# The first four up products of a fused attention and two-layer network, moved into the hand-pinned opening order

## The chip, the cores and the metric

The kernel runs on one core of a Trainium2 chip. The metric is the device time of one execution in microseconds (us), as the median of several runs. The core has a matrix engine (PE in the profile, with its weight loads listed as PEld), a vector engine (DVE), a scalar engine for activations (ACT), a general engine (POOL), and queues that start DMA transfers (SPq). Each engine works through its own list of instructions in order, and waits on semaphores that the others raise.

## The reference

Attention between `x` (4 batches, 8 heads, 512 rows, 64 columns) and a `state` of 32 rows per head goes into two gated layers, each of 512 to 2048 to 512 features:

```python
a = softmax(scale * x @ state.T)            # per head; xread below
xread = a @ state
sread = softmax(scale * state @ x.T) @ x    # state reads x
x = concat([xread, sread])                  # 4 * (512 + 32) tokens, 512 features
h = x @ moe_w_in;   y = (h - tanh(h)) @ moe_w_out
h = y @ moe2_w_in;  out = (h * tanh(log1p(exp(min(h, 20))))) @ moe2_w_out
```

Two things of it shape the kernel. All inputs are stored as 64-bit floats, so each weight arrives as pairs of 32-bit words and has to be converted on the chip. And `xread @ w_in` is computed as `a @ (state @ w_in)`: the small product `state @ w_in` is made first, per batch, and the softmax weights `a` multiply it directly.

## The kernel before, in words

**Layer one.** A batch has 512 tokens; they are the moving columns of nearly every matmul (128x512). The 2048 hidden features are 16 tiles `t` of 128. An *up product* of tile `t` (`up_x`, line 525) makes `h`, 128 features by 512 tokens, in one PSUM bank: for each of two halves `j` of the heads, three matmuls (`mm3p`, line 503) on rounded operands split in a high and a low part, `swh`/`swl` being the split of `state @ w_in` and `ath`/`atl` that of the transposed softmax weights `a`. So an up product is six matmuls. `elem1` (line 515) then makes `t = h - tanh(h)`: a Tanh on ACT, a subtraction on DVE, and, from tile 3 on, a further split in `gh` (ACT) and `gl` (DVE). A *down product* of tile `t` (`down_x`, line 548) adds `t` times `w_out` into four accumulators, PSUM banks a0 to a3; tiles 0 to 2 of batch 0 (`PLAIN = 3`) use plain 32-bit matmuls, `acc<-t,w`, and later tiles the three-matmul form.

**Weights.** Each load brings 512 KB of 64-bit weights into one of six staging buffers (`st` three times, `wide` three times). A conversion (`conv_steps`, line 189) is a pair on ACT, a Prelu that writes `w` and a Copy that writes `r`, and then one SCALAR_TENSOR_TENSOR on DVE that joins them in `w`. The Copy frees the staging buffer, and the next load is issued only then (`load_next`, line 174). Layer one needs 16 conversions of `w_in` (key `("w1i", c, k)`, chunk `c` of four feature tiles, piece `k`) and 16 of `w_out` (`("w1o", t)`). They are loaded alternately after the first five.

**State times w_in.** For chunk 0 it is made feature tile by feature tile (`sw_first`, line 489): eight small matmuls `swp<-w,sbt` of 128 columns, the high part `swh` by two ACT copies, the low part `swl` by two DVE subtractions (`sw_first_lo`). For later chunks it is one piece (`sw`, line 475) of 512 columns, which needs all four converted pieces of the chunk.

**Order.** The work of the opening is written out by hand in `FIRST_STEPS` (line 34): a letter and a number for a step, for instance `w3` for the next step of converting piece 3, `f2` and `g2` for the high and low part of `state @ w_in` of feature tile 2, `h1`/`l1` for the parts of `a`. Up to the bar `|` each instruction of PE, ACT and DVE is pinned behind the one before it on its engine (class `Pinned`; its line 59 issues nearly every instruction, so nearly every row of the profile says L59). Behind the bar only a floor holds: nothing may go ahead of the last pinned instruction, and a scheduler orders the rest by its own rules when the program is built. The main loop (line 958) then issues, per step `i`, the up product of step `i`, its side work, and the down product of step `i - 3`:

```python
    for s in range(16):
        at(s, lambda s=s: conv_w1o(s))
        if s < 11:
            at(s, lambda s=s: conv_w1i((s + 5) // 4, (s + 5) % 4))
            if s % 4 == 2:
                at(s, lambda s=s: sw(0, s // 4 + 1))
```

So step `s` converts `w_out` tile `s` and `w_in` piece `s + 5`, and `sw(0, 1)` comes at step 2. Piece 4, which is (1, 0), is converted by the last steps `w4 w4 w4` of the table.

**Banks.** Up products use h0 and h1 in turn. The small products of the opening take their bank from a rotating list (`side_bank`, line 129), and step `z` moves the place in that list.

Of the kernel before, what the change touches and what calls it, by code (L numbers as in the profile page):

```python
# [29 lines left out]

FIRST_LOADS = "s0123wwt4567wwww"
FIRST_STEPS = """
    k4 s0 x0 X0 x1 X1 x2 X2 x3 X3 w0 w0 c0 C0 C1 k2 w0 t0 m0 t1 w1 w1 f0 b0 p0 P0 m1 e0 p1 P1 b1
    p2 e1 P2 u0 p3 P3 v0 y0 k6 w2 u1 v1 w2 h0 z2 q1 y1 h1 g0 l0 w1 l1 Q0 Q1 | f1 g1 w2 f2 g2
    w3 w3 w3 f3 g3 w4 w4 w4
"""
BLOCKS = [4, 4, 4, 3, 2]

# [31 lines left out]
def attention_moe_kernel(  # L72
# [11 lines left out]
    B, H, S, D = x.shape  # L84
# [5 lines left out]
    T = S + NS  # L90
# [9 lines left out]
    TE, AC, V = (Pinned(e, order) for e in (nc.tensor, nc.scalar, nc.vector))  # L100
# [18 lines left out]
    def put(*units):  # L119
        for u in units:  # L120
            if u.slot is None:
                halves.append(u)
            else:
                free.append(u.slot)

    ps_n = [0]
    banks = ["s0", "s1", "a0", "a1", "a2", "a3", "h0", "h1"]
# [129 lines left out]
    X, A, AT = {}, {}, {}  # L257
# [20 lines left out]
    def xt_t(b, k):  # L278
        P["x", b, k] = ps = side_bank("xtp")
        for r in range(4):  # L280
            TE.transpose(
                out=ps[:, r * 128:(r + 1) * 128],
                in_=X[b, k].t[:, r * 128:(r + 1) * 128],
                identity=ident,
            )

    def xt_c(b, k):
        XT[b, k] = get("xt")
        evac(XT[b, k].t, P.pop(("x", b, k)), 0 if b else k)
# [157 lines left out]
    def at_a_hi(b, j):  # L447
        ps = side_bank("atp")
        a = A.pop((b, j))
        for r in range(4):  # L450
            TE.transpose(
                out=ps[:, r * 128:(r + 1) * 128],
                in_=a.t[:, r * 128:(r + 1) * 128],
                identity=ident,
            )
        put(a)
        h = get("ath", F32R)
        last[0] = AC.activation(out=h.t, in_=ps, func=ACTF.Copy).ins
        AT.setdefault(b, []).append((h, ps))

    def at_a_lo(b, j):
        h, ps = AT[b][j]
        l = get("atl", F32R)
        V.tensor_tensor(out=l.t, in0=ps, in1=h.t.bitcast(F32), op=ALU.subtract)
        AT[b][j] = (h, l)
# [7 lines left out]
    SW = {}  # L473
# [29 lines left out]
    def mm3p(o, lh, ll, rh, rl, start, stop):  # L503
        TE.matmul(out=o, lhsT=lh, rhs=rh, start=start, stop=False)
        TE.matmul(out=o, lhsT=lh, rhs=rl, start=False, stop=False)
        TE.matmul(out=o, lhsT=ll, rhs=rh, start=False, stop=stop)
# [4 lines left out]
    def h_bank(tags):  # L511
        h_n[0] += 1
        return psum.tile([128, 512], F32, tag=tags[h_n[0] % len(tags)], name="h")

    def elem1(key, h):
        t = get("t")
        last[0] = AC.activation(out=t.t, in_=h, func=ACTF.Tanh).ins
        V.tensor_tensor(out=t.t, in0=h, in1=t.t, op=ALU.subtract)
        if key[0] == 0 and key[1] < PLAIN:
            G[key] = t  # L520
            return
        G[key] = split(t.t, name="g")
        put(t)

    def up_x(b, t):
        h = h_bank(["h0", "h1"])
        c, f = t // 4, (t % 4) * 128
        for j in range(2):
            wh, wl = SW[b, c, j]
            ah, al = AT[b][j]  # L530
            mm3p(h, wh.t[:, f:f + 128], wl.t[:, f:f + 128], ah.t, al.t, j == 0, j == 1)
        if t % 4 == 3:
            for j in range(2):
                put(*SW.pop((b, c, j)))
        if t == NT - 1:
            for p in AT.pop(b):
                put(*p)
        elem1((b, t), h)

    def acc_bank(i, tags=("a0", "a1", "a2", "a3")):  # L540
        return psum.tile([128, 512], F32, tag=tags[i % len(tags)], name=f"acc{i}")
# [115 lines left out]
    def up_2(n, t, i_tail):  # L657
        N = 128 * len(blocks[n])
        h = h_bank(HT)[:, :N]
        c, f = t // 4, (t % 4) * 128  # L660
        for k in range(KD):
            wh, wl = W2I[c, k]
            yh, yl = YB[n][k]
            mm3p(
                h, wh.t[:, f:f + 128], wl.t[:, f:f + 128], yh.t[:, :N], yl.t[:, :N],
                k == 0, k == KD - 1,
            )
        if t == NT - 1:
            for p in YB.pop(n):
                put(*p)  # L670
        if n == 0 and done[0] < len(late):
            e, r = get("e"), get("r")
            m, rr = e.t[:, :N], r.t[:, :N]
        else:
            e, r = None, stage.tile([128, 1024], F32, tag="st", name="er")
            m, rr = r[:, :N], r[:, 512:512 + N]
        AC.activation(out=m, in_=h, func=ACTF.Exp)
        if i_tail is not None:
            elem2_hi(*i_tail)
        V.tensor_scalar(out=m, in0=m, scalar1=E20, scalar2=None, op0=ALU.min)  # L680
        V.scalar_tensor_tensor(
            out=m, in0=m, scalar=2.0, in1=m, op0=ALU.add, op1=ALU.mult
        )
        AC.activation(out=rr, in_=m, func=ACTF.Ln, bias=2.0)
        AC.activation(out=rr, in_=rr, func=ACTF.Exp, scale=-1.0)
        E2[n, t] = (e, r, m, rr, h, N)

    def elem2(n, t, i_tail):
        e, r, m, rr, h, N = E2[n, t]
        w = get("w2")  # L690
        ww = w.t[:, :N]
        V.scalar_tensor_tensor(
            out=ww, in0=m, scalar=2.0, in1=rr, op0=ALU.add, op1=ALU.mult
        )
        if i_tail is not None:
            elem2_lo(*i_tail)
        V.tensor_tensor(out=rr, in0=h, in1=rr, op=ALU.mult)
        V.scalar_tensor_tensor(
            out=m, in0=ww, scalar=2.0, in1=m, op0=ALU.subtract, op1=ALU.mult
        )  # L700
        V.scalar_tensor_tensor(
            out=m, in0=m, scalar=-1.0, in1=rr, op0=ALU.mult, op1=ALU.mult
        )
        put(w)

    def elem2_hi(n, t):
        e, r, m, rr, h, N = E2[n, t]
        gh = get("gh", F32R)
        AC.activation(out=gh.t[:, :N], in_=m, func=ACTF.Copy)
        G["2", n, t] = (gh, get("gl", F32R))  # L710

    def elem2_lo(n, t):
        e, r, m, rr, h, N = E2.pop((n, t))
        gh, gl = G["2", n, t]
        V.tensor_tensor(
            out=gl.t[:, :N], in0=m, in1=gh.t[:, :N].bitcast(F32), op=ALU.subtract
        )
        if e is not None:
            put(e, r)
# [150 lines left out]
    st = {}  # L870
    for key in FIRST_LOADS:
        if key in "st":
# [18 lines left out]
            first[f] = conv_steps(("w1i", f // 4, f % 4))  # L891
        W1I[f // 4, f % 4] = next(first[f])

    def skip_banks(n):
        ps_n[0] += n

    steps = {
        "x": lambda k: xt_t(0, k), "X": lambda k: xt_c(0, k), "s": lambda j: state_t(j, st[j]),
# [1 line left out]
        "m": lambda j: sc_max(0, j), "b": lambda j: sc_sub(0, j), "e": lambda j: sc_exp(0, j),  # L900
        "u": lambda j: nm_sum(0, j), "v": lambda j: nm_rec(0, j), "y": lambda j: nm_mul(0, j),
        "h": lambda j: at_a_hi(0, j), "l": lambda j: at_a_lo(0, j), "f": sw_first,
        "g": sw_first_lo, "z": skip_banks,
        "w": conv_first, "k": keep_warm, "p": lambda k: xt_t(1, k), "P": lambda k: xt_c(1, k),
        "q": sc_m, "Q": lambda j: sc_c(1, j),
    }
# [18 lines left out]
    def up(q):  # L925
        if q[0] == "x":
            up_x(q[1], q[2])
        elif q[0] == "s":
            up_s(q[1])
        else:  # L930
            if q[2] == 0:
                if q[1] == 0:
                    pre = nc.scalar.preload_act_table_set("natural_log_exp_and_others").ins
                    order(pre, last[0])
                    AC.last, V.last = pre, None
                    AC.floor = V.floor = None
                    AC.on = V.on = True
                y_block(q[1])

    def down(q):  # L940
        if q[0] == "x":
            down_x(q[1], q[2])
        elif q[0] == "s":
            down_s(q[1])
        else:
            down_2(q[1], q[2])
# [10 lines left out]
    for i in range(len(seq) + 2):  # L957
        marks.append([e.recent for e in engines])
        q = seq[i] if i < len(seq) else None
        prev = [seq[i - k][1:] if start["2"] <= i - k < len(seq) else None for k in range(3)]  # L960
        if q:
            up(q)
        if prev[0]:
            up_2(*prev[0], prev[2])
        elif prev[2]:
            elem2_hi(*prev[2])
        if prev[1]:
            elem2(*prev[1], prev[2])
        elif prev[2]:
            elem2_lo(*prev[2])  # L970
        if prev[0] and q[2] >= NT - 6:
            y_block(q[1] + 1, YSPARE)
        for f in side.pop(i, []):
            f()
        while low < len(seq) and low <= i - ahead(i):
            down(seq[low])
            low += 1
        pinned = AC.on, V.on
        AC.on = V.on = False
        late_conv(i)  # L980
        AC.on, V.on = pinned
# [33 lines left out]
```

## Time and profile before

| what | us |
|---|---|
| time, median of 3 runs (lowest, highest) | 745.51 (744.6, 745.74) |
| time of the profiled execution | 744.79 |
| span of the profiled execution | 743.0 |
| PE busy in the span | 729.0 (98%) |
| DVE busy | 542.8 (73%) |
| ACT busy | 413.4 (56%) |

The span runs from the first to the last instruction of the program; the execution's own time is a little longer. Busy time overlaps between engines. A row of the timeline gives the start, the length, the engine, the line, the operation, what is written and read, the shape, how many records were merged, and in brackets how long the engine had stood idle before it and which engine and tile ended that. The 32-bit matmuls `acc<-t,w`, `swp` and `sbp` leave two records for each instruction.

### The profile page before, as it was taken

The page shows a single profiled execution, that of the slowest core. Times are in us where ns is not written, and L with a number is a line of the kernel's source. Part 1 is how long each engine was busy: PE and PEld are TensorE (multiplying, and loading weights), DVE is VectorE, ACT ScalarE, POOL GpSimd, SP SyncE. Part 2 cuts the span into 40 slices and gives each one's busy share as a digit, 9 for nine tenths or more (in the row PEclk, how much of TensorE's full clock was granted, in tenths as well). Part 3 has the DMA queues.
Part 4 walks back from the last instruction along what each step waited for, and adds up shares of the span by engine and source line. Part 5 has one row for each costly group of instructions (what it writes and reads, how often), then busy time and mean ns, then how long its engine had stood idle before and what let it go on. Part 6 is the DMA issues. An engine that isn't in the chain of part 4 may idle for free.

```text
span 743.0 us, 10599 instructions
## 1 busy us (share of the span) xinstructions
PE 729.0 (98%) x4144; PEld 591.9 (80%) x4144; DVE 542.8 (73%) x1006; ACT 413.4 (56%) x770; POOL 6.6 (1%) x14
## 2 busy tenths in 40 slices
PE   8899999999999999999999999999999999999997
PEld 6467876788767898778888888888888888898996
DVE  5899655834466343777698988878788788888896
ACT  6998544534555443787674654535454454545563
POOL 0000010001000000000000000000000000000000
PEclk9999999999999999999999999999999999999999
DMA  9984110002100110453310000100010000100100
GB/s 295 328 298 141 58 56 1 2 24 78 43 29 13 47 57 1 142 169 115 114 56 1 1 1 16 42 0 1 0 57 1 0 1 1 56 1 2 43 1 28
DMA packets 17169, 43.14 MB, mean 58 GB/s; under 512 B 2656, under 2 KB 6752, under 8 KB 17120
## 3 DMA queue, kind: packets, MB, share of 16 engines
q1 hardware_dynamic: 16480, 40.38, 16.3%
q0 software_dynamic: 640, 2.10, 0.9%
q8 instruction: 32, 0.52, 0.3%
q14 instruction: 17, 0.14, 0.1%
HBM read 38.01 MB, written 4.46 MB: 57 GB/s over the span
## 4 chain that ended last, share of the span: by engine, by line
PE 89%; ACT 6%; DVE 3%; DMA 1%; issue 0%; SPq 0%; ACTq 0%
PE acc L59 46%; PE h L59 37%; ACT w L59 2%; PE swp L59 2%; ACT r L59 2%; PE srd L59 1%; DMA x<-in_x_dram 1%; ACT swh L59 1%; PE xtp L59 1%; PE sct L59 1%; DVE swl L59 1%; ACT t L59 1%; PE atp L59 1%; PE e2p L59 1%; DVE gl L59 0%
## 5 line engine op out<-in xcount | busy, mean ns | idle before, releaser
L59 PE MATMUL h<-yl,wh 128*128 128x512 f32 (+2 forms) x320 | 114.5, 358 | 0.0
L59 PE MATMUL h<-yh,wl 128*128 128x512 f32 (+2 forms) x320 | 114.4, 358 | 0.0
L59 PE MATMUL h<-yh,wh 128*128 128x512 f32 (+2 forms) x320 | 114.4, 358 | 0.0
L59 PE MATMUL acc<-wh,gl 128*128 128x512 f32 x288 | 112.6, 391 | 0.0
L59 PE MATMUL acc<-wl,gh 128*128 128x512 f32 x288 | 112.5, 391 | 0.0
L59 PE MATMUL acc<-wh,gh 128*128 128x512 f32 x288 | 112.5, 391 | 0.0
L59 ACT ACTIVATE er<-er 128x512 f32<-128x512 f32 (+2 forms) x136 | 75.7, 557 | 42.8 <-DVE er L59 40.6
L59 PE MATMUL acc<-gh,wh 128*128 128x512 f32 x244 | 98.9, 405 | 0.0
L59 PE MATMUL acc<-gh,wl 128*128 128x512 f32 x244 | 95.7, 392 | 0.0
L59 PE MATMUL acc<-gl,wh 128*128 128x512 f32 x244 | 95.5, 391 | 0.0
L59 ACT ACTIVATE er<-h 128x512 f32<-128x512 f32 (+2 forms) x68 | 35.5, 522 | 103.7 <-PE h L59 102.6
L59 DVE SCALAR_TENSOR_TENSOR er<-er 128x512 f32<-128x512 f32 (+2 forms) x136 | 81.3, 598 | 4.7
L59 PEld LDWEIGHTS h<-yl,wh 128*128 128x128 f32 x320 | 60.3, 188 | 9.4 <-DVE yl L59 0.7
L59 PEld LDWEIGHTS h<-yh,wh 128*128 128x128 f32 x320 | 60.3, 188 | 9.1 <-ACT yh L59 0.3
L59 PEld LDWEIGHTS h<-yh,wl 128*128 128x128 f32 x320 | 60.3, 188 | 7.4
L59 PEld LDWEIGHTS acc<-wh,gl 128*128 128x128 f32 x288 | 54.0, 188 | 12.0 <-DVE gl L59 0.7
L59 PEld LDWEIGHTS acc<-wh,gh 128*128 128x128 f32 x288 | 54.1, 188 | 11.1 <-ACT t L59 0.8
L59 PEld LDWEIGHTS acc<-wl,gh 128*128 128x128 f32 x288 | 54.1, 188 | 10.3
L59 PEld LDWEIGHTS acc<-gh,wh 128*128 128x128 f32 x244 | 45.8, 188 | 16.0 <-issue 4.4
L59 DVE TENSOR_TENSOR t<-h,t 128x512 f32<-128x512 f32 x48 | 33.0, 687 | 34.9 <-ACT t L59 34.8
L59 DVE TENSOR_SCALAR er<-er 128x512 f32<-128x512 f32 (+2 forms) x68 | 25.8, 379 | 44.3 <-ACT er L59 44.1
L59 PEld LDWEIGHTS acc<-gl,wh 128*128 128x128 f32 x244 | 45.9, 188 | 10.4 <-issue 2.1
(145 smaller groups left out, 1233.7 us busy)
## 6 DMA issues: line engine op xcount, KB each, us to landing
st<-in_moe_w_in_dram SPq DMA_DIRECT2D x27, 512.0 KB, 4.3
st<-in_moe_w_out_dram SPq DMA_DIRECT2D x22, 512.0 KB, 3.8
wide<-in_moe_w_out_dram SPq DMA_DIRECT2D x10, 512.0 KB, 4.9
out_dram<-wide SPq DMA_DIRECT2D x16, 256.0 KB, 2.2
wide<-in_moe_w_in_dram SPq DMA_DIRECT2D x5, 512.0 KB, 6.0
x<-in_x_dram SPq DMA_DIRECT2D x8, 256.0 KB, 5.8
x<-in_x_dram POOLq DMA_DIRECT2D x6, 256.0 KB, 3.1
wide<-in_x_dram POOLq DMA_DIRECT2D x2, 256.0 KB, 3.2
```

Source lines behind the costliest of these rows:

```text
L59: i = fn(*args, **kw)
```

## The change

The four up products of tiles 0 to 3 of batch 0 leave the main loop, which now starts its up products at step 4, and become steps of the pinned table: `U` opens an up product and issues its first half, `V` issues its second half, `T` issues the Tanh chain. Tiles 0 and 1 keep the banks h1 and h0; tiles 2 and 3 take the accumulators' banks a2 and a3. The remaining steps of chunk 0 (`f1` to `g3`) and the conversion of piece (1, 0) are pinned too, the bar moves to the end of the table, and the step `z` now names the next bank instead of skipping some. `up_x` is cut in two helpers with the same matmuls.

```diff
-    p2 e1 P2 u0 p3 P3 v0 y0 k6 w2 u1 v1 w2 h0 z2 q1 y1 h1 g0 l0 w1 l1 Q0 Q1 | f1 g1 w2 f2 g2
...
+    p2 e1 P2 u0 p3 P3 v0 y0 k6 w2 u1 v1 w2 h0 z0 q1 y1 z5 h1 g0 l0 U0 w1 l1 w3 w3 z2 f1 V0 w2 g1 T0
...
+    z4 f2 w3 U1 V1 g2 z2 f3 T1 U2 V2 g3 T2 U3 V3 Q0 Q1 T3 w4 w4 w4 |
...
     def up_x(b, t):
         h = h_bank(["h0", "h1"])
+        for j in range(2):
+            up_half(b, t, h, j)
+        up_end(b, t, h)
+
+    def up_half(b, t, h, j):
         c, f = t // 4, (t % 4) * 128
-        for j in range(2):
-            wh, wl = SW[b, c, j]
-            ah, al = AT[b][j]
-            mm3p(h, wh.t[:, f:f + 128], wl.t[:, f:f + 128], ah.t, al.t, j == 0, j == 1)
+        wh, wl = SW[b, c, j]
+        ah, al = AT[b][j]
+        mm3p(h, wh.t[:, f:f + 128], wl.t[:, f:f + 128], ah.t, al.t, j == 0, j == 1)
+
+    def up_end(b, t, h):
         if t % 4 == 3:
             for j in range(2):
-                put(*SW.pop((b, c, j)))
+                put(*SW.pop((b, t // 4, j)))
...
-    def skip_banks(n):
-        ps_n[0] += n
+    def up_first(t):
+        H[t] = acc_bank(t) if t > 1 else h_bank(["h0", "h1"])
+        up_half(0, t, H[t], 0)
+
+    H = {}
+
+    def next_bank(i):
+        ps_n[0] = i + len(banks) - 1
...
-        "g": sw_first_lo, "z": skip_banks,
+        "g": sw_first_lo, "z": next_bank, "U": up_first,
+        "V": lambda t: up_half(0, t, H[t], 1), "T": lambda t: up_end(0, t, H[t]),
...
-        if q:
+        if q and i >= 4:
             up(q)
```

Two places show what the built programs make of this. The first is PE's list around the first down product, `acc_502` to `acc_505` being the four accumulators; before:

```order
L59 MATMUL acc_502<-t,w 128x512
L59 MATMUL acc_503<-t,w 128x512
L59 MATMUL h<-ath,swh 128x512
L59 MATMUL h<-atl,swh 128x512
L59 MATMUL h<-ath,swl 128x512
L59 MATMUL h<-ath,swh 128x512
L59 MATMUL h<-atl,swh 128x512
L59 MATMUL h<-ath,swl 128x512
L59 MATMUL acc_504<-t,w 128x512
L59 MATMUL acc_505<-t,w 128x512
L59 MATMUL swp<-w,sbt 32x512 x8
```

The same place now, `acc_402` being the up product of tile 3 in bank a3:

```order
L60 MATMUL acc_402<-ath,swl 128x512
L60 MATMUL acc_502<-t,w 128x512
L60 MATMUL acc_503<-t,w 128x512
L60 MATMUL acc_504<-t,w 128x512
L60 MATMUL acc_505<-t,w 128x512
L60 MATMUL swp<-w,sbt 32x512 x8
L60 MATMUL acc_502<-t,w 128x512
L60 MATMUL h<-ath,swh 128x512
L60 MATMUL h<-atl,swh 128x512
L60 MATMUL acc_503<-t,w 128x512
```

The up product of tile 3 stood inside the first down product and is now ahead of it; the work ahead of the `swp` of chunk 1 is the same in both lists. Behind it, one more product of the second down product comes after the next up product has begun.

The second place is ACT's list from the two copies of `ath` on, where `w` and `r` are the Prelu and the Copy of a conversion; before:

```order
L59 ACTIVATE ath<-atp 128x512 x2
L59 ACTIVATE scs<-sct 128x2x128 x2
L59 ACTIVATE w<-wide 128x512
L59 ACTIVATE swh<-swp 128x128 x2
L59 ACTIVATE r<-wide 128x512
L59 ACTIVATE w<-wide 128x512
L59 ACTIVATE r<-wide 128x512
L59 ACTIVATE t<-h 128x512
L59 ACTIVATE swh<-swp 128x128 x2
L59 ACTIVATE w<-wide 128x512
L59 ACTIVATE swh<-swp 128x128 x2
L59 ACTIVATE r<-wide 128x512
```

The same place now, `acc_390` and `acc_402` being the up products of tiles 2 and 3:

```order
L60 ACTIVATE ath<-atp 128x512 x2
L60 ACTIVATE w<-wide 128x512
L60 ACTIVATE r<-wide 128x512
L60 ACTIVATE swh<-swp 128x128 x2
L60 ACTIVATE t<-h 128x512
L60 ACTIVATE swh<-swp 128x128 x4
L60 ACTIVATE t<-h 128x512
L60 ACTIVATE t<-acc_390 128x512
L60 ACTIVATE scs<-sct 128x2x128 x2
L60 ACTIVATE t<-acc_402 128x512
L60 ACTIVATE gh<-t 128x512
L60 ACTIVATE w<-wide 128x512
```

The second conversion in these rows, that of piece (1, 0), stood ahead of the first Tanh and now stands behind the fourth Tanh and `gh`; all later conversions follow it, eight pairs without anything between them.

## Rows read from the trace of the kernel before

**Rows 1.** Waits of PE, whole span: total us, times, longest.
```profile
PE swp L59 <- DVE w L59: 2.4, 2, 1.6
PE h L59 <- DVE t L59: 1.3, 1, 1.3
PE h L59 <- ACT swh L59: 0.3, 1, 0.3
```
**Rows 2.** Windows: us, busy of each engine, granted clock, DMA share, GB/s.
```profile
20.00:57.00 37.00, 34.18 (x200) 20.46 (x199) 32.95 (x60) 36.93 (x75) 0.00 (x0) 1.00 0.90 308
738.00:740.00 2.00, 1.02 (x5) 0.52 (x3) 0.69 (x1) 0.60 (x1) 0.00 (x0) 1.00 0.07 27
740.00:743.00 3.00, 0.00 (x0) 0.00 (x0) 0.00 (x0) 0.00 (x0) 0.00 (x0) 0.67 0.42 157
```
**Rows 3.** Timeline of PE from 3 to 69 us.
```profile
3.46 1.98 PE L59 MATMUL sbp<-ident,stt 128*64 128x128 f32 x16
...
21.30 0.40 PE L59 MATMUL h<-ath,swl 128*128 128x512 f32 x1
22.52 0.45 PE L59 MATMUL swp<-w,sbt 64*32 64x128 f32 x16 [0.82 <-DVE w L59]
23.21 0.72 PE L59 MATMUL swp<-w,sbt 64*32 64x128 f32 x16 [0.24 <-PE swp L59]
25.21 0.47 PE L59 MATMUL h<-ath,swh 128*128 128x512 f32 x1 [1.28 <-DVE t L59]
...
28.02 1.88 PE L59 MATMUL acc<-t,w 128*128 128x512 f32 x4
...
32.93 1.09 PE L59 MATMUL swp<-w,sbt 64*32 64x512 f32 x16
...
36.28 0.50 PE L59 MATMUL h<-ath,swh 128*128 128x512 f32 x1 [0.34 <-ACT swh L59]
...
38.27 1.09 PE L59 MATMUL sbp<-ident,stt 128*64 128x128 f32 x16
...
68.50 1.09 PE L59 MATMUL swp<-w,sbt 64*32 64x512 f32 x16 [1.55 <-DVE w L59]
```
**Rows 4.** Timeline of ACT from 19 to 34 us.
```profile
19.42 0.60 ACT L59 ACTIVATE ath<-atp 128x512 fp32r<-128x512 f32 x1 [1.07 <-PE atp L59]
...
21.87 0.68 ACT L59 ACTIVATE w<-wide 128x512 f32<-128x512 f32 x1
...
23.01 0.60 ACT L59 ACTIVATE t<-h 128x512 f32<-128x512 f32 x1
23.49 0.46 ACT L59 ACTIVATE swh<-swp 128x128 fp32r<-128x128 f32 x2
...
25.21 0.73 ACT L59 ACTIVATE w<-st 128x512 f32<-128x512 f32 x1
25.77 0.74 ACT L59 ACTIVATE r<-st 128x512 uint32<-128x512 uint32 x1
...
33.37 0.74 ACT L59 ACTIVATE gh<-t 128x512 fp32r<-128x512 f32 x1
33.88 0.80 ACT L59 ACTIVATE w<-st 128x512 f32<-128x512 f32 x1
```
**Rows 5.** Timeline of DVE from 23 to 69 us.
```profile
23.98 0.49 DVE L59 TENSOR_TENSOR swl<-swp,swh 128x128 fp32r<-128x128 f32 x2
24.38 0.68 DVE L59 TENSOR_TENSOR t<-h,t 128x512 f32<-128x512 f32 x1
...
27.66 0.69 DVE L59 SCALAR_TENSOR_TENSOR w<-w,r 128x512 uint32<-128x512 uint32 x1 [0.43 <-ACT r L59]
...
67.66 1.29 DVE L59 SCALAR_TENSOR_TENSOR w<-w,r 128x512 uint32<-128x512 uint32 x2
```
**Rows 6.** DMA from 20 to 57 us: rate in 40 slices; issues, KB, us to landing.
```profile
GB/s 403 381 244 244 350 186 275 248 319 270 239 221 261 425 425 425 416 399 416 372 354 297 279 368 345 297 199 204 226 252 314 297 301 239 363 350 283 345 159 323
...
wide<-in_moe_w_out_dram SPq DMA_DIRECT2D x9, 512.0 KB, 4.9
st<-in_moe_w_in_dram SPq DMA_DIRECT2D x6, 512.0 KB, 5.7
```

More of the change, by code (lines that the diff above doesn't have):

```diff
@@ L35 @@
     k4 s0 x0 X0 x1 X1 x2 X2 x3 X3 w0 w0 c0 C0 C1 k2 w0 t0 m0 t1 w1 w1 f0 b0 p0 P0 m1 e0 p1 P1 b1
-    p2 e1 P2 u0 p3 P3 v0 y0 k6 w2 u1 v1 w2 h0 z2 q1 y1 h1 g0 l0 w1 l1 Q0 Q1 | f1 g1 w2 f2 g2
-    w3 w3 w3 f3 g3 w4 w4 w4
+    p2 e1 P2 u0 p3 P3 v0 y0 k6 w2 u1 v1 w2 h0 z0 q1 y1 z5 h1 g0 l0 U0 w1 l1 w3 w3 z2 f1 V0 w2 g1 T0
+    z4 f2 w3 U1 V1 g2 z2 f3 T1 U2 V2 g3 T2 U3 V3 Q0 Q1 T3 w4 w4 w4 |
 """
```

## The prediction

> **What bounds the kernel now.** I read the page first: PE is busy for 98% of the span, so time can only come from PE's few waits or be lost in new ones. The list of PE's waits over the whole span names them [rows 1], and the timeline of PE shows where they lie [rows 3]: 0.82 and 0.24 us before the two `swp` at 22.5 and 23.2 us, 1.28 before the `h` at 25.21, 0.34 at 36.28, and 1.55 before the `swp` at 68.50. These five sum to 4.23 us; the first three, 2.34 us, lie where the change works. The reader should then look at the other engines in that stretch, for a wait of PE is only the late end of something. From 20 to 57 us ACT is busy 36.93 of 37.00 us, while PE has 34.18 [rows 2]. ACT bounds this stretch: it has the conversions of all first-layer weights to do, and it has no hole. PE's waits here are ACT's order showing through. Whoever changes that order must ask first whether ACT gets a hole.
>
> **The change part by part.** No matmul, activation or vector instruction is added or removed; a few merged rows differ, not the work. Split helpers and the new bank step cost no instruction, so these edits cost 0. The two up products in banks a2 and a3 add one wait: the first down product may write there only when the Tanh chain of tiles 2 and 3 has read them. By the walk below that chain is through at 28.7 us and the down product starts at 32.4, so this wait is covered by 3.7 us; it would cost only if the chain came later than the weight.
>
> What counts is the order. ACT now stands, in pinned order, behind each step of a ping-pong: PE's up product, ACT's Tanh, DVE's subtraction, and, because DVE's list puts the conversion of piece 3 behind the first subtraction, PE's next `swp`. Nothing may fill ACT's waits, since all other conversions are behind the table. I walk the new lists with durations of rows, starting where nothing has moved:
>
> The `ath` copy is at 19.42 and the up product of tile 0 ends at 21.30 + 0.40 = 21.70 as before [rows 3, 4]. Tanh, 0.60 long [rows 4], to 22.3. Subtraction, 0.68 [rows 5], to 23.0; the joining instruction behind it starts 0.60 after it did and takes 0.69 [rows 5], to 23.65. The `swp` of feature tile 3, 0.45 [rows 3], to 24.15. Two `swh` copies, 0.46 [rows 4], to 24.65, the second Tanh overlapping them, to 25.1. Its subtraction ahead of the `swl` pair, 0.68 and 0.49 with an overlap of 0.1 as at 23.98 [rows 5], to 26.25. PE has meanwhile done the rest and now needs four more matmuls for tile 3; by the 0.23 us from one to the next and 0.40 for the last, to 27.3. Tanh to 27.95, subtraction to 28.7, `gh`, after which ACT is free 0.52 later (33.37 to 33.88 [rows 4]): 29.25.
>
> So the conversion of piece (1, 0) begins at 29.25; before it began at 21.87 [rows 4]. From 20.0 to 29.25 ACT has a conversion pair (1.12, two steps of 0.56 [rows 4]), six small copies (three times 0.33), four Tanh (four times 0.49), two `scs` (0.54) and `gh` (0.52): 5.1 us of work in 9.25, thus a hole of some 4.1 us in an engine that had none.
>
> What PE does meanwhile: its matmuls end at 27.3, and the first down product needs `w_out` tile 0, the second conversion in the new order. Four steps of 0.56 from 29.25, the last 0.7 long, end at 31.65; DVE's 0.69 ends at 32.35; PE starts at 32.4. That is a new wait of about 5.1 us. The joins on DVE are not the bound: with 1.12 between Copies and 0.60 to 0.69 each they keep up.
>
> Then PE does four products of about 0.9 (28.02: two in 1.88 [rows 3]) until 36.0, and meets the `swp` of chunk 1, which needs pieces (1, 0) to (1, 3): the seventh pair in the new list. Its Copy starts at 29.25 + 13 x 0.56 = 36.5, ends 37.2, joined at 37.95: PE goes on at 38.0 after 2 us of waiting. Before, the same `swp` stood at 32.93 with the same work ahead of it, so PE is 5.1 us late here. Next, ACT copies `swh` only after nine pairs and a Prelu, at 39.9, with another Copy between the two: the second ends at 41.55, PE's `h` starts at 41.7 after another 1.8. With six matmuls and one product more, the `sbp` that was at 38.27 [rows 3] comes at 44.0: 5.7 us late.
>
> From there to the `swp` at 68.50 PE has the same work, and before it waited 1.55 there. The weight it waited for was joined at 67.66 [rows 5], kept late by DVE's list. PE now arrives at 66.95 + 5.7, about 72.6 (0.9 sooner at the `swp`, which stands four matmuls earlier in its list), so some 4 us lie between that join and PE even if DVE were no earlier. I count the 1.55 as gained. What costs it if the cover goes: DVE later by 4 us.
>
> Moved DMAs: each Copy releases the next load, so the load behind piece (1, 0) is issued about 30.5 instead of 23.16, and it is the load of piece (1, 3). Loads take 4.9 to 5.7 us to land here [rows 6], so it lands between 35.4 and 36.2, and ACT wants it at 36.0. This is the tightest place: from no cost to 0.2. The following loads are asked for every 1.12 us, which is 524 KB / 1.12 us = 468 GB/s, while no slice of this stretch shows more than 425 [rows 6]. At 425 a load takes 1.23, 0.1 behind ACT with each; at the mean of 308 [rows 2] it would take 1.7, 0.6 behind with each, over the two or three loads that matter before PE's `h` up to 1.5 us. I take 0.1, nearest to the slices in which the queue is full, and keep 0 and 1.5. The SP queue holds nothing else then, so nothing is delayed behind a waiting load.
>
> The sum: 5.7 late, less 1.55, is +4.15; with 0.1 for the loads +4.25. ACT's hole of 4.1 us says the same in another way. The profiled execution took 744.79, so 749.0; it lies 0.72 below the median of the runs shown, from which it would be 749.8. I forecast 749.4.
>
> **The clock.** The granted clock is 1.00, its level of 2.4 GHz, in the stretches shown with PE at work; at the very end, PE having stopped in the stretch from 738 to 740, it falls: 0.67 as the mean of the last three us, so its lower level within them [rows 2]. A gap of 5 us like the new one occurs nowhere inside the run (the longest listed is 1.6 us [rows 1]), so no row shows whether it would fall there. The Trainium skill, in TensorE: Matmul & The Clock Gate, section "HAM oscillation — how this bites in real kernels", says that a long wait between bursts of matmuls puts the clock back to half and lets the next burst run cold; by that rule the gap would cost more than itself. The price from rows: the 16 records of `sbp` took 1.98 at the start and 1.09 later [rows 3], a factor of 1.8, which I take for the lower level though no row gives the clock there. Four products would then take 6.6 from 32.4, to 39.0 instead of 36.0, of which 2 fall into the wait for the `swp`; that ends 1.9 later at 40.9, the next product at 42.5, against 41.7: 0.8 us more. If the clock rises again during the four products, nothing; if it stays low through the next up product and the product behind it, 0.8 x 2.3 = 1.8 on top, 2.6 in all.
>
> **The rivals.**
> 1. The clock falls in the gap and costs: +0.8, from just above 0 to 2.6, thus 750.2. For it: the fall at the end of the run; against: the next two waits, 2 and 1.8 us, take most of it.
> 2. Loads come late: ACT then waits for transfers in its row of bare conversions; up to +1.5, typical +0.8, thus 750.2. For it: 468 GB/s asked; against: the six loads ahead of that of piece (1, 3) have long landed.
> 3. On the other side: the pinned up products fill PE's holes and no new wait takes their place. All five waits go, 4.23 us: 744.79 - 4.23 = 740.6. It needs the conversion of (1, 0) to start early: since each us that ACT starts later is one us for PE, break-even is at 29.25 - 4.25 = 25.0, which would take round trips of half the length that the rows show. For it only that PE does have the up products to do in its 2.34 us of holes; against it ACT's 36.93 of 37.
> 4. The change is neutral: ACT's hole is partly filled and what PE loses is given back at 68.5: 745.5. Against it: the pinned list leaves nothing to fill with.
>
> **How the numbers follow.** Forecast 53%, rival 1 18%, rival 2 15%, rival 3 6%, rival 4 8%. A measurement of this kernel tells about 0.2%, 1.5 us, from no change. Slower takes the first three and a little of the fourth's spread, 0.87; same 0.07; faster 0.06. The range leaves out rivals 3 and 4 and reaches, above, to the forecast with 2.6 more: 746.9 to 752.3, where the lower end stands for round trips 2.5 us shorter than I walked.
>
> **What would show it.** Right: an idle time of some 5 us of PE before the first `acc<-t,w`, ended by DVE's `w`; two more, near 2 us, before the `swp` of chunk 1 and the `h` behind it; ACT idle some 4 us between 20 and 29; no wait at the `swp` near 72. Wrong: ACT busy throughout from 20 to 30, or the first down product before 30. The clock's granted share in the window from 30 to 45 decides rival 1; ACT waiting for DMA after 35 decides rival 2.

## The result, and the profile after

The changed kernel takes 749.89 us (median of 4, 749.15 to 750.28) against 745.06 us of the kernel before, run beside it (median of 4): a ratio of 1.006, 95% interval 1.0047 to 1.0072. That is 4.83 us slower; forecast were 749.4 us and a loss of 4.25. The profiled execution took 750.14 us with a span of 748.4, 5.4 more than the span before.

The waits of PE between 18 and 80 us in the changed kernel (total us, times, longest) are these two, in place of the five of [rows 1]:

```profile
PE acc L60 <- DVE w L60: 5.1, 1, 5.1
PE h L60 <- ACT swh L60: 1.7, 1, 1.7
```

The waits of ACT between 18 and 60 us. Before, the same view had only the wait for `atp`, 1.1 us:

```profile
ACT swh L60 <- PE swp L60: 1.8, 1, 1.8
ACT t L60 <- PE acc L60: 1.1, 2, 0.6
ACT ath L60 <- PE atp L60: 1.0, 1, 1.0
ACT w L60 <- DMA st<-in_moe_w_in_dram: 0.9, 1, 0.9
ACT gh L60 <- DVE t L60: 0.8, 1, 0.8
ACT t L60 <- PE h L60: 0.3, 1, 0.3
```

Windows of the changed kernel (columns as in [rows 2]):

```profile
20.00:57.00 37.00, 30.08 (x167) 15.53 (x167) 28.45 (x52) 32.11 (x65) 0.00 (x0) 0.91 0.75 271
20.00:30.00 10.00, 7.44 (x71) 4.38 (x70) 7.07 (x17) 6.13 (x17) 0.00 (x0) 1.00 0.42 163
25.00:30.00 5.00, 2.57 (x11) 1.52 (x9) 3.51 (x8) 3.18 (x7) 0.00 (x0) 1.00 0.00 2
32.00:36.00 4.00, 3.33 (x4) 1.51 (x5) 2.60 (x4) 4.00 (x8) 0.00 (x0) 0.50 0.88 287
33.00:38.00 5.00, 5.00 (x7) 1.90 (x7) 3.33 (x5) 5.00 (x10) 0.00 (x0) 0.50 0.92 302
38.50:46.00 7.50, 5.82 (x40) 2.56 (x40) 5.85 (x10) 6.60 (x13) 0.00 (x0) 1.00 1.03 415
```

ACT, busy for 36.93 of these 37 us before, now has 32.11: a hole of 3.87 us between 20 and 30, and the wait of 0.93 us for a load later. Loads stop too: from 25 to 30 us the core moved 2 GB/s, from 33 to 38 us 302, and only then over 400. And in the stretch from 32 to 36 the granted clock is 0.50, its level of 1.2 GHz.

PE's timeline, to be held against [rows 3]:

```profile
27.18 0.40 PE L60 MATMUL acc<-ath,swl 128*128 128x512 f32 x1
32.67 6.47 PE L60 MATMUL acc<-t,w 128*128 128x512 f32 x8 [5.10 <-DVE w L60]
39.07 1.09 PE L60 MATMUL swp<-w,sbt 64*32 64x512 f32 x16
...
42.90 0.50 PE L60 MATMUL h<-ath,swh 128*128 128x512 f32 x1 [1.68 <-ACT swh L60]
...
45.35 1.09 PE L60 MATMUL sbp<-ident,stt 128*64 128x128 f32 x16
...
73.01 1.09 PE L60 MATMUL swp<-w,sbt 64*32 64x512 f32 x16
```

The up products end at 27.6, the first down product starts 5.10 us later, its four products take 6.47 us, and the `swp` at 73.01, which stood at 68.50, has no wait. The `sbp` that stood at 38.27 stands at 45.35, 7.1 us late; less the 1.55 that went at the last `swp`, 5.5 remain, near the difference of the spans.

ACT's timeline, to be held against [rows 4]:

```profile
24.46 0.45 ACT L60 ACTIVATE swh<-swp 128x128 fp32r<-128x128 f32 x2 [1.75 <-PE swp L60]
...
28.96 0.63 ACT L60 ACTIVATE gh<-t 128x512 fp32r<-128x512 f32 x1 [0.76 <-DVE t L60]
29.50 0.65 ACT L60 ACTIVATE w<-wide 128x512 f32<-128x512 f32 x1
...
39.38 0.69 ACT L60 ACTIVATE w<-st 128x512 f32<-128x512 f32 x1 [0.93 <-DMA st<-in_moe_w_in_dram]
...
41.23 0.58 ACT L60 ACTIVATE swh<-swp 128x512 fp32r<-128x512 f32 x1
```

The conversion of piece (1, 0), at 21.87 before, begins at 29.50.

### The profile page after: what moved, and what is told of

The parts are those of the page before. It is cut to its first block, busy times and chain, and to the rows that moved or that the text cites. A ratio compares the mean times of both kernels' runs of the same rounds, so it can differ in the third digit from the quotient of the medians.

```text
span 748.4 us, 10596 instructions
## 1 busy us (share of the span) xinstructions
PE 732.0 (98%) x4144; PEld 592.9 (79%) x4144; DVE 543.6 (73%) x1006; ACT 414.0 (55%) x770; POOL 6.6 (1%) x14
## 4 chain that ended last, share of the span: by engine, by line
PE 93%; DVE 3%; ACT 2%; DMA 2%; issue 0%; SPq 0%; ACTq 0%
PE acc L60 49%; PE h L60 38%; PE swp L60 2%; PE srd L60 1%; DMA st<-in_moe_w_in_dram 1%; DMA x<-in_x_dram 1%; DVE swl L60 1%; PE xtp L60 1%; PE e2p L60 1%; PE sct L60 0%; ACT w L60 0%; PE sc L60 0%; ACT swh L60 0%; PE atp L60 0%; ACT r L60 0%; DVE a L60 0%
## 5 line engine op out<-in xcount | busy, mean ns | idle before, releaser
L60 PEld LDWEIGHTS acc<-gh,wl 128*128 128x128 f32 x244 | 45.8, 188 | 10.3 <-issue 0.4
```

Source lines behind the costliest of these rows:

```text
L60: i = fn(*args, **kw)
```

## The experiments

The theory to be tested: the pinned table makes ACT wait for PE and DVE in turn with nothing allowed to fill these waits, the conversions of the weights come later by that hole, and PE pays it at the first down product. Its rivals: the up products in the accumulators' banks make the down product wait; PE's lower clock costs by itself; the loads, released later, bind. Each result is a ratio to the kernel before, run on the same chip.

**The bar ahead of the last Tanh chain.**

```diff
-    ... g3 T2 U3 V3 Q0 Q1 T3 w4 w4 w4 |
+    ... g3 T2 U3 V3 Q0 Q1 | T3 w4 w4 w4
```

> The changed kernel with the bar two steps earlier, ahead of the Tanh chain of tile 3 and of the conversion of piece (1, 0), so that both are left to the scheduler. Theory of the hole in ACT: the pin on the last chain is what keeps the conversions back, so the wait of PE before the first down product falls from 5.1 to about 3 us and the total comes about 3 us under the changed kernel, near 746.5. Theory of the banks (the accumulators' banks make the down product wait for tiles 2 and 3): nothing moves, 749.9, and the wait stays near 5 us. Theory of the clock: only as far as the shorter gap leaves the clock at its upper level, about 1 us, 748.9.

Measured: 746.7 us, ratio 1.0018 (1.0008 to 1.0029). Two steps less under the pin take back 3.2 us of the loss in the median. The twelve executions differ by their mean granted clock: three had 0.995, as all four of the changed kernel had, and took 747.6 to 748.4 us; four had 0.999 or 1.000 and took 745.3 to 746.1. So 1.5 to 2.3 us come back at the clock of the changed kernel, and 3.8 to 4.6 where the clock stayed up. The profiled execution is one of the three (747.74). PE's wait in its timeline, and a wait of ACT:

```profile
30.29 9.04 PE L60 MATMUL acc<-t,w 128*128 128x512 f32 x14 [3.17 <-DVE w L60]
```

```profile
40.44 0.60 ACT L60 ACTIVATE swh<-swp 128x512 fp32r<-128x512 f32 x1 [1.47 <-PE swp L60]
```

Tiles 2 and 3 are still in a2 and a3, so the banks did not make most of the loss. The clock is not ruled out by this run. It still falls (0.70 from 30 to 40 us), and in this order it is on the path: seven products (14 records) stand ahead of the `swp` here instead of four, they take 9.04 us, and ACT waits 1.47 us for the `swp`.

**The bar behind f2.**

```diff
-    z4 f2 w3 U1 V1 g2 ... Q0 Q1 T3 w4 w4 w4 |
+    z4 f2 | w3 U1 V1 g2 ... Q0 Q1 T3 w4 w4 w4
```

> The changed kernel with the bar behind f2: the up product of tile 0, its Tanh chain, f1 and f2 stay pinned, everything behind is free. Theory of the hole: ACT is busy again from 23 us on, PE's wait before the first down product is under 1 us, and the time falls below the kernel before by 1 to 2.5 us, near 743. Theory of the banks: tiles 2 and 3 are still in a2 and a3, so the loss stays, near 749.9.

Measured: 742.45 us, ratio 0.9969 (0.9957 to 0.9981); in a second run beside another kernel 742.93, ratio 0.9963 (0.9951 to 0.9975), for which was expected:

> The same kernel as the one with the bar behind f2, run beside the version with two banks so that the two share a chip: 742.4 within 0.6 us.

This version beats both kernels. Its window from 20 to 30 us, and all waits of PE between 18 and 80 us:

```profile
20.00:30.00 10.00, 9.76 (x61) 5.40 (x60) 8.72 (x19) 9.69 (x24) 0.00 (x0) 1.00 0.79 286
```

```profile
PE sc L60 <- DVE swl L60: 0.6, 1, 0.6
PE h L60 <- ACT swh L60: 0.4, 1, 0.4
PE h L60 <- DVE swl L60: 0.3, 1, 0.3
PE swp L60 <- DVE w L60: 0.3, 1, 0.3
```

ACT is busy 9.69 of 10 us again instead of 6.13, and PE waits 1.5 us in all, against 4.2 before [rows 1] and 6.8 in the changed kernel. A part of the gain that rival 3 of the prediction hoped for (4.23 us) is there, as soon as the pin ends early enough. Its executions had mean granted clocks of 0.999 and 1.000; against the twelve executions of the kernel before that had 1.000 on the same chip (median 744.4) the gain is 2.0 us, and the rest of the difference to their common median goes with the clock.

**Conversions put into ACT's holes, all still pinned.** New steps `o` convert tiles of `w_out`; the main loop leaves out what the table has done.

```diff
-    z4 f2 w3 U1 V1 g2 z2 f3 T1 U2 V2 g3 T2 U3 V3 Q0 Q1 T3 w4 w4 w4 |
+    z4 f2 w3 w4 w4 o0 U1 V1 g2 z2 f3 T1 w4 o0 U2 V2 g3 T2 o0 w5 U3 V3 Q0 Q1 w5 T3 w5 |
```

> The changed kernel, all pinned as before to its bar, with conversion steps of piece (1, 0), w_out tile 0 and piece (1, 1) put into the places of the table where ACT waits. Theory of the hole: the holes of ACT between 20 and 29 us shrink from 4 to about 1 us and PE's first wait to under 1 us; about 4.5 us under the changed kernel, near 745. Theory that pinning itself costs (PE's ping-pong with ACT and DVE): the ping-pong only gets longer, 749.9 or more.

Measured: 743.81 us, ratio 0.9983 (0.9974 to 0.9991), 6 us under the changed kernel. Its window:

```profile
20.00:30.00 10.00, 9.04 (x75) 5.23 (x76) 7.80 (x18) 8.78 (x22) 0.00 (x0) 1.00 0.83 287
```

The table is pinned to its end and the time falls all the same: it is not the pinning that costs but that ACT has nothing pinned into its waits. PE's wait at the first down product is 0.29 us. The granted clock is 1.00 from 20 to 40 us, so this run by itself does not part the hole from the clock; the run with seventeen extra matmuls below does. Against the executions of the kernel before with a mean granted clock of 1.000 (median 744.4) the gain is 0.6 us.

**The banks alone, in the kernel before.**

```diff
     def up_x(b, t):
-        h = h_bank(["h0", "h1"])
+        h = acc_bank(t) if b == 0 and t in (2, 3) else h_bank(["h0", "h1"])
```

> The kernel before with one part of the change alone: up products of tiles 2 and 3 of batch 0 write the accumulators' banks a2 and a3; no step is added to the pinned table. Theory of the hole: no loss, the wait of 1.28 us for a bank may go, 0 to 1 us under the kernel before, near 744.5. Theory of the banks: the first down product waits for the chains of tiles 2 and 3 and the time rises by 2 us or more.

Measured: 744.48 us, ratio 0.9992 (0.9983 to 1.0001): no loss, and no gain that can be told from none. The first down product has no wait in this run's trace, so the theory of the banks falls. The `h` wait of 1.28 us is gone, and a wait of 1.0 us in the same place, of the up product of tile 2 for ACT, has come.

**Extra matmuls in PE's wait, the rest of the order the same.**

```diff
-    ... Q0 Q1 T3 w4 w4 w4 |
+    ... Q0 Q1 T3 K6 w4 w4 w4 |
```

`K6` is six matmuls of 128 columns on constant data into bank h1, added work that the output doesn't use.

> The changed kernel with six extra matmuls on constant data (1.5 us by the row of the same matmuls near 15 us) at the start of PE's wait of 5.1 us; the order of all other instructions is the same. They take nothing from the kernel's own work, and the idle part of the wait falls to about 3.6 us. Theory that the lower clock of the profile of the changed kernel costs by itself: if the clock stays up, four down products take 3.6 instead of 6.5 us and the time falls by 1 us or more, to 748.9 or below. Theory that the loads bind behind the wait (ACT waited 0.93 us for a load at 39.4 us and set the next up product): the down products may be faster, but PE then waits longer for ACT, and the time stays within 0.3 us of 749.9. If the clock falls all the same, nothing is told apart and the time is 749.9.

Measured: 749.82 us, ratio 1.0057 (1.0042 to 1.0072), not to be told from the changed kernel. PE's timeline:

```profile
32.86 5.37 PE L60 MATMUL acc<-t,w 128*128 128x512 f32 x8 [3.76 <-DVE w L60]
38.33 1.09 PE L60 MATMUL swp<-w,sbt 64*32 64x512 f32 x16
...
42.66 0.50 PE L60 MATMUL h<-ath,swh 128*128 128x512 f32 x1 [2.18 <-ACT swh L60]
...
46.55 1.22 PE L60 MATMUL sbp<-ident,stt 128*64 128x128 f32 x16
```

The clock fell here too (0.65 from 32 to 36 us), so the time of the run does not separate the theories as it was meant to. Its rows show two things. The `swp` behind the down products began 0.7 us earlier than in the changed kernel, and PE's next wait grew from 1.68 to 2.18: behind the first fall ACT sets the pace. Behind that wait the clock fell a second time:

```profile
44.00:46.00 2.00, 2.00 (x6) 1.19 (x4) 1.64 (x3) 1.56 (x3) 0.00 (x0) 0.50 1.02 410
```

The `h` began 0.24 us earlier than in the changed kernel, the `sbp` behind the same work 1.20 us later: this fall, with PE never waiting, cost 1.4 us, and the span is 1.3 us longer. The profiled execution is the slowest of six (748.43 to 751.48 us), so the others need not have had the second fall.

**Seven and seventeen extra matmuls.** From seven on, the free instructions behind 33 us come in another order, so these two are compared with each other.

> As the run before with seven matmuls (1.75 us). From seven on the scheduler orders the free instructions behind 33 us in another way, so this is the partner for the run with seventeen and not for the changed kernel. Both theories: a clock fall as in the changed kernel if the remaining idle time of 3.4 us still brings one; time between 748.5 and 750.

> As the run before with seventeen matmuls (4.25 us), which leave PE idle for about 0.9 us; otherwise the same order as with seven. The granted clock should stay at its upper level. If the clock costs by itself, this is 1 us or more under the run with seven; if the loads and ACT bind, the two are within 0.4 us of each other, and PE's wait before the next up product is longer by what the down products gain.

Measured: 749.17 us, ratio 1.0042 (1.0029 to 1.0056), with seven; 747.70 us, ratio 1.0031 (1.0020 to 1.0042), with seventeen. The intervals overlap, so 1.5 us between the medians is likely, not certain. Of the five executions with seven, the one with a mean granted clock of 1.000 took 747.32 us, like those with seventeen (all 0.999 or 1.000), and the two with 0.995 took 749.5. PE's timeline with seven:

```profile
32.20 9.10 PE L60 MATMUL acc<-t,w 128*128 128x512 f32 x14 [3.54 <-DVE w L60]
41.23 1.09 PE L60 MATMUL swp<-w,sbt 64*32 64x512 f32 x16
...
45.96 1.09 PE L60 MATMUL sbp<-ident,stt 128*64 128x128 f32 x16
```

and with seventeen:

```profile
32.18 6.25 PE L60 MATMUL acc<-t,w 128*128 128x512 f32 x14 [1.35 <-DVE w L60]
38.35 1.09 PE L60 MATMUL swp<-w,sbt 64*32 64x512 f32 x16
42.27 0.50 PE L60 MATMUL h<-ath,swh 128*128 128x512 f32 x1 [0.92 <-ACT swh L60]
...
44.14 1.09 PE L60 MATMUL sbp<-ident,stt 128*64 128x128 f32 x16
```

With the clock kept up (1.00 from 28 to 40 us, against 0.50 from 32 to 36 with seven) the same 14 records take 6.25 instead of 9.10 us: 2.85 us gained, of which 0.92 goes into a wait for ACT and some 1.8 arrive at `sbp`. In that order three more products stand ahead of the `swp`, so PE and not ACT sets the pace there.

The run with seventeen also shows what the hole costs without a fall of the clock. ACT is as idle as in the changed kernel (busy 6.26 of the 10 us from 20 to 30), the clock stays up, and 747.70 us are still some 3.3 above the three executions of the kernel before that had a mean granted clock of 1.000 on the same chip (744.3 to 744.6).

**The ACT pair of piece (1, 0) in the longest hole.**

```diff
-    z4 f2 w3 U1 V1 g2 z2 f3 T1 U2 V2 g3 T2 U3 V3 Q0 Q1 T3 w4 w4 w4 |
+    z4 f2 w3 w4 w4 U1 V1 g2 z2 f3 T1 U2 V2 w4 g3 T2 U3 V3 Q0 Q1 T3 |
```

> The changed kernel with the ACT pair of piece (1, 0) put into ACT's longest hole (1.75 us, behind f2) and its DVE step behind the third up product; the table stays pinned to its end. It frees one staging buffer some 6 us earlier. Hole theory alone, by the same walk as in the prediction: ACT's free conversions begin about 0.55 us earlier, and the time falls by 0.7 us, to 749.2. If the load that ACT waited for also cost its 0.93 us, the fall is about 1.6 us, to 748.3, and ACT's wait for a DMA is gone.

Measured: 748.46 us, ratio 1.0038 (1.0025 to 1.0051), 1.4 us under the changed kernel, nearer to the second figure; its five executions had the same mean granted clock of 0.995. PE's timeline and ACT's wait for a load:

```profile
31.89 5.67 PE L60 MATMUL acc<-t,w 128*128 128x512 f32 x8 [3.99 <-DVE w L60]
...
41.29 0.50 PE L60 MATMUL h<-ath,swh 128*128 128x512 f32 x1 [1.67 <-ACT swh L60]
```

```profile
ACT w L60 <- DMA st<-in_moe_w_out_dram: 0.2, 1, 0.2
```

The down products run at the lower clock here too (0.51 from 32 to 36), and still the next up product comes 1.6 us earlier: 0.8 from the first down product's start on, and the rest with ACT's wait for the load, 0.2 instead of 0.9.

**The version with the bar behind f2, tiles 2 and 3 in h0 and h1.**

```diff
-        H[t] = acc_bank(t) if t > 1 else h_bank(["h0", "h1"])
+        H[t] = h_bank(["h0", "h1"])
```

> The kernel with the bar behind f2, and tiles 2 and 3 in h0 and h1 like the others instead of in a2 and a3. If the extra banks are what made that version faster than the kernel before, the wait of PE for the Tanh chain of tile 0 comes back (1.3 us) and the time is near 743.7. If the order alone did it (the early up product of tile 0 and the free conversions behind the bar), nothing changes: 742.4 within 0.6 us.

Measured: 742.49 us, ratio 0.9958 (0.9944 to 0.9971), the same as its partner with four banks. The extra banks are not needed for the gain.

## Why the prediction was right, point by point

- **ACT bounds the stretch, and a hole in it is the price.** Forecast: 4.1 us idle between 20.0 and 29.25. Measured: 3.87 between 20 and 30. Three edits that only give ACT work or freedom (bar ahead of the last chain, fill, bar behind f2) brought 3.2, 6 and 7 us back. The clock has a share in these sums, but the hole does not need it: with seventeen extra matmuls the clock stayed up, the hole stayed too, and so did 3.3 us of loss.
- **The first wait.** Conversions from 29.25, first down product at 32.4 after 5.1 us; measured 29.50, 32.67 and 5.10. The ping-pong could be walked from rows of before, since no engine in it met anything new.
- **The banks cost nothing.** As the banks alone showed, within its interval, and the version with two banks (742.49 against 742.93).
- **The gain at the last `swp`.** Counted as 1.55; the wait is gone, so it is.
- **The step that was undersized is the one on the moved loads.** The prediction took 0.1 us, "nearest to the slices in which the queue is full"; ACT waited 0.93 us for the load of its ninth pair. No load was issued from 21.2 to 30.7 us. The first two behind that landed in 4.0 and 4.1 us, so the load of piece (1, 3), the prediction's "tightest place", was in time. The third, issued at 32.93, took 6.4, and the five after it 6.6 to 7.3. While the third was under way the core moved some 302 GB/s (33 to 38 us), not the 425 of the best slices but close to the mean of 308, which the prediction had priced at 0.6 us with each load and had not taken. What came is what rival 2 described, with its typical 0.8. With this wait and a start of the conversions that was 0.25 later, ACT's `swh` copy came at 41.23 instead of 39.9, and PE's `h` at 42.90 instead of 41.7; that is most of the 1.1 us between the forecast loss and that of the two profiles, and the run with the early pair takes it back.
- **The clock fell, as rival 1 had it, and in the profiled execution it is not on the path.** The down products took 6.47 us (forecast 6.6 at the lower level) and the 2 us wait before the `swp` was swallowed whole. But the `swp` ended at 40.2, and ACT's copy that waited for it started only at 41.23, because of the load. Without the wait of 0.93 ACT would have come to this copy at 40.3, just after the `swp` had ended. The run with the early pair bears this out: the clock is low (0.51), the load is nearly in time, and PE still waits 1.67 us for ACT. So the 0.8 us of rival 1 are not in this execution. Where PE sets the pace a fall does cost: 1.4 us for the second fall in the run with six extra matmuls, some 1.8 between seven and seventeen. The rule of the Trainium skill (TensorE: Matmul & The Clock Gate, section "HAM oscillation — how this bites in real kernels"), that a long wait between bursts lets the next one run cold, agrees with 0.50 in the window behind the gap; that such a gap costs more than itself does not show in this order's time. All four executions of the changed kernel had a mean granted clock of 0.995, so no run has this very order with the clock kept up, and this stays a reading of rows.
- **Two numbers were nearer than their working.** The walk from the profile of before gave 749.0 and the profiled execution took 750.14, 1.1 more; the forecast of 749.4 comes within 0.5 of the median partly by luck, since it was put midway between two starting points. And the loss of 4.83 us is smaller than the 5.4 between the profiles probably because the median of the kernel before holds executions with a lower clock (last section). The upper end of the range, 752.3, is 0.3 above its own sum, 749.4 + 2.6; nothing hangs on it.
- **Rival 3 was wrong for this kernel and right about the holes.** Under the pin PE's five waits became two longer ones. With the pin ended behind f2 they shrank to 1.5 us, and 2.7 us of span were gained.

## What to carry to other kernels

Before a hand-written order is made longer, look at which engine has no idle time in that stretch: each place where that engine waits inside the new order needs other work of its own put there by hand, or the order has to end earlier, so that a scheduler can put it there. Filling the waits of the engine that shows them (here PE's 2.3 us) is worth nothing if the engine behind them gets a hole. A moved step that frees a buffer also moves the loads behind it, and loads that are asked for one behind the other after a hole should be priced at the mean rate of the stretch (here 308 GB/s, measured 302), not at its best slices. And before a difference of medians is put down to an edit, the mean granted clocks of the executions should be set beside each other: here they go with up to 2.6 us within one kernel.

## What the runs showed of the hardware

The granted clock fell to its lower level in smaller gaps than the one of 5.10 us: in the run with the bar ahead of the last chain PE had stood idle 3.17 us. In the kernel with the banks alone it fell with no wait over 1.0 us near it. Its windows:

```profile
22.00:24.00 2.00, 0.91 (x32) 0.40 (x32) 1.76 (x5) 2.00 (x7) 0.00 (x0) 0.93 0.87 324
24.00:27.00 3.00, 2.75 (x7) 2.21 (x8) 2.44 (x6) 3.00 (x8) 0.00 (x0) 0.50 0.81 276
```

PE was busy for 0.91 of the 2 us ahead of the fall, with small `swp` matmuls and waits of 0.81, 0.24 and 0.96 us; in the profiled execution of the kernel before, with waits of 0.82, 0.24 and 1.28 in the same place, the granted clock from 20 to 57 us was 1.00 [rows 2, 3].

The order alone does not settle it, for executions of one and the same kernel differ. Of 29 executions of the kernel before on one chip, twelve had a mean granted clock of 1.000 over the span and took 744.0 to 745.2 us, four had 0.995 and took 746.5 to 747.3, and the other thirteen, at 0.996 to 0.998, took 745.2 to 746.3; of the eleven with the banks alone, the clocks run from 0.997 to 1.000. A lower clock goes with up to 2.6 us here (medians 744.4 and 747.0). Where in the span it fell in executions without a trace is not known, and that the fall makes all of these 2.6 us is not shown.
